# First cells of a fused mLSTM and gated MLP kernel: other PSUM banks for two products, another order on ScalarE, and cell 4's exponents between two weight joins

## The chip, the cores and the metric

The kernel runs on one core of one Trainium2 chip. The metric is the device time of one execution in microseconds. An execution is also recorded by the hardware profiler; the span of the recorded instructions is a little shorter than the time of that execution, and every position in the trace below is counted from the span's start. The five engines of a core have queues of their own and run side by side: PE (matrix products; its weight loads are a row of their own, PEld), DVE (VectorE), ACT (ScalarE), POOL (GpSimd) and SP (which here only issues DMAs). An engine works its instructions off in the order of its queue, and an instruction that waits for a semaphore holds up everything behind it on that engine.

## The reference

For batch 4, 8 heads, 768 steps and head size 40, an mLSTM cell is run step by step, and its output goes through an MLP whose gate is a cosine:

```python
m_new = np.maximum(f_gate[t] + m, i_gate[t])
f_stab, i_stab = np.exp(f_gate[t] + m - m_new), np.exp(i_gate[t] - m_new)
C = f_stab * C + i_stab * outer(v[t], k[t])
n = f_stab * n + i_stab * k[t]
y[t] = sigmoid(o_gate[t]) * (C @ q[t]) / np.maximum(np.abs(n @ q[t]), 1.0)
...
h = x @ w_in                  # x: y as (3072, 320); w_in (320, 2048)
out = (h * np.cos(h)) @ w_out # w_out (2048, 320)
```

## The kernel before

**Cells.** The recurrence is computed in chunks of 128 steps. A chunk of one batch entry is a cell: cell n is chunk n // 4 of batch entry n % 4, and there are 24. Inside a cell the decay between two steps is a 128x128 matrix per head, so that the cell becomes attention-like products. A cell's parts are functions that record instructions:

- `turn(n)` (L421) transposes q and k on PE into PSUM, and `turn_out(n)` (L432) copies both to SBUF, on ACT, or with k on DVE (L434, L436, L438).
- `decay_exponents(n)` (L370): DVE takes the exponents of all 8 heads from E, a 512 KB tile that SP loaded (`load_E`, L345), at L372; POOL puts the causal mask on it (L373). `decay(n)` (L380) takes the exponential on ACT (L381). Cells 0 and 1 get their exponents through PE instead: `wall_in` and `spread` write a mask and the maxima into PSUM banks (L352, L359).
- `scores(n)` (L440) multiplies k and q on PE, `weigh(n)` (L450) multiplies by the decay on DVE (L453, two instructions), `values(n)` (L466) multiplies by v on PE (L472), and `normalize(n)` (L525) makes z on DVE (L535 to L548).
- `weigh_k(n)` makes kw on POOL (L394). `seam(n)` (L569) transposes z into PSUM (px, L575) and forms the increment of the state (pu, L582); `seam_out(n)` (L590) copies px to xT, the MLP's input, and `state(n)` (L592) puts pu into the state (L596 copies it for cells 0 to 3). Both are ACT copies in the first four cells.

**The MLP.** Four cells make a chunk of 512 columns. `Up` (L603) multiplies it by two blocks of w_in: two products for each of two 128-row pieces (L617) and two for the last 64 rows (L620). `near` (ACT, L625), `rest` (DVE, L628), `sin` (ACT, L633) and `gate` (DVE, L637) make h cos h from it, and `down` multiplies by w_out (L750 in the first chunk, L693 later). The next `Up` reuses the two PSUM banks of the one before, so it waits for both gates.

**Weights.** They arrive as 64-bit numbers and are made into 32-bit ones: `parts` (ACT, L138 and L140) splits a piece and `join` puts it together (DVE, L144, L146, L148, then L149 on POOL or, with `nc.vector`, on DVE). The rounds of both_parts join the pieces as they need them. The first three pieces of w_in are joined in `first_cells`, the first piece of w_out in `cell_after_first` through `out_parts` and `out_join` (L890, L894).

**PSUM.** Eight banks: two of pool `ps_a` (tag "a", even cells), four of `ps_o` (tag "o", odd cells), two of `ps_u`. Tiles of one tag take its banks in turn, and a tile waits until the readers of the tile that had the bank are done. The two banks of `ps_u` are first `pw`, into which `warm(k)` (L759) writes k products of zeros that keep PE busy, and `pmu`, which holds the mask of cell 0; then they go to `Up`.

**Order.** Nothing reorders: under a manual schedule the order of the calls is the order on every engine. `first_cells` (L764) writes out cells 0 to 3 by hand. Then `both_parts(c, b)` (L899) does a round for each batch entry of a chunk: an `Up`, a cell's scores, `down` of the round before, the cell's values, another `Up`, and so on. In the first round `cell_after_first` (L874) is called inside the first `Up`, between its first and second pair of products: it turns cell 4 and takes its exponents, its decay and the first join of w_out. `gates_exp` (L259, two exponentials L261 on ACT and a DMA of the result to DRAM on POOL's queue, L262) and `gates_diagonal` (L264, one DVE product, L266) prepare what `gates_turn` (L269) gives to the later chunks.

Of the kernel before, what the change touches and what calls it, by code (L numbers as in the profile page):

```python
# [11 lines left out]
FP = mybir.dt.float32  # L12
# [17 lines left out]
def kernel(  # L30
# [22 lines left out]
    B, H, S, D = q.shape  # L53
    C = 128
    NC = S // C
    BH = B * H
    HP = H // 2
    D1 = D + 1
# [5 lines left out]
    NK = DM // 128  # L64
# [78 lines left out]
    def join(dst, hi, t, m, last=None):  # L143
        nc.vector.tensor_scalar(out=t.bitcast(FP), in0=t.bitcast(FP), scalar1=LEAST, scalar2=GREATEST,  # L144
                                op0=OP.max, op1=OP.min)
        nc.vector.tensor_scalar(out=t, in0=t, scalar1=5, scalar2=2, op0=OP.logical_shift_left,  # L146
                                op1=OP.logical_shift_right)
        nc.vector.scalar_tensor_tensor(out=t, in0=hi, scalar=TOP2, in1=t, op0=OP.bitwise_and, op1=OP.bitwise_or)  # L148
        (last or nc.gpsimd).tensor_tensor(out=dst.bitcast(I32), in0=t, in1=m, op=OP.add)  # L149
# [61 lines left out]
    def gates_in():  # L211
        nc.sync.dma_start(out=F0, in_=fg[:, 0:C])
        nc.scalar.dma_start(out=a0, in_=ig[:, 0:C])

    def later_gates_in():
        nc.sync.dma_start(out=F1.rearrange("r c s -> r (c s)"), in_=fg[:, C:])
        nc.sync.dma_start(out=a1.rearrange("r c s -> r (c s)"), in_=ig[:, C:])
# [41 lines left out]
    def gates_exp():  # L259
        for e in (eG, eW):  # L260
            nc.scalar.activation(out=e, in_=e, func=AF.Exp)  # L261
        nc.gpsimd.dma_start(out=G_d, in_=eG.rearrange("r c s -> r (c s)"))  # L262

    def gates_diagonal():  # L264

        nc.vector.tensor_tensor(out=dd, in0=ident[0:BH, 0:BH].unsqueeze(1).to_broadcast([BH, R - 1, BH]),  # L266
                                in1=eG[:, 0:R - 1, last].to_broadcast([BH, R - 1, BH]), op=OP.mult)
# [40 lines left out]
    def sigmoid(c, bs=slice(0, B)):  # L308
        o = sig[c][:, bs.start * DM:bs.stop * DM]
        nc.scalar.activation(out=o, in_=o, func=AF.Sigmoid)  # L310
# [51 lines left out]
    def psum_o():  # L362
        return ps_o.tile([128, HP, C], FP, name="pm", tag="o")

    def cols(n, j, width):
        c, b = divmod(n, B)
        return tab[:, c, j, ts(b, H)].unsqueeze(2).to_broadcast([128, H, width])


    def decay_exponents(n):  # L370
        E = Es[n]
        nc.vector.tensor_tensor(out=E, in0=E, in1=cols(n, 0, C), op=OP.subtract)  # L372
        nc.gpsimd.affine_select(out=E, in_=E, compare_op=OP.is_ge, fill=1.0e30, base=0,  # L373
                                pattern=[[0, H], [1, C]], channel_multiplier=-1)
# [16 lines left out]
    def weigh_k(n):  # L391
        if n < N - B:
            kw = p2.tile([128, H, D], FP, name="kw", tag="kw")
            nc.gpsimd.tensor_tensor(out=kw, in0=ks[n % NB][:, :, 0:D], in1=cols(n, 1, D), op=OP.mult)  # L394
            kws[n] = kw

    def psum(n):

        return (ps_o, "o") if n < B and n % 2 == 1 else (ps_a, "a")
# [32 lines left out]
    def turn_out(n, on_dve=True):  # L432
        qT, kT = qkT[n]
        nc.scalar.copy(out=qT, in_=pts[n][0])  # L434
        if on_dve:
            nc.vector.tensor_copy(out=kT, in_=pts[n][1])  # L436
        else:
            nc.scalar.copy(out=kT, in_=pts[n][1])  # L438
# [11 lines left out]
    def weigh(n):  # L450
        for j in range(2):
            w = Es[n].rearrange("p (a j) t -> p a j t", j=2)[:, :, j]
            nc.vector.tensor_tensor(out=w, in0=pss[n][j], in1=w, op=OP.mult)  # L453
# [12 lines left out]
    def values(n):  # L466
        pool, tag = psum(n)
        ph = pool.tile([128, H, D1], FP, name="ph", tag=tag)
        for j in range(2):
            for p in range(HP):  # L470
                h = 2 * p + j
                nc.tensor.matmul(ph[:, h], Es[n][:, h], vs[n % NB][:, h], start=True, stop=True)  # L472
        heads_of[n] = heads_of.get(n), ph
# [95 lines left out]
    def seam(n):  # L569

        pool, tag = psum(n)
        if n < TURNED:
            px = pool.tile([128, NK + 1, C], FP, name="px", tag=tag)
            for i in range(NK + 1):
                nc.tensor.transpose(px[:, i], ys[n][:, ts(i, 128)], ident)  # L575
            pxs[n] = px
        if n < N - B:

            pu = pool.tile([128, HP, D1], FP, name="pu", tag=tag)
            for p in range(HP):  # L580
                for j in range(2):
                    nc.tensor.matmul(pu[64 * j:64 * j + D, p], kws[n][:, 2 * p + j], vs[n % NB][:, 2 * p + j],  # L582
                                     start=True, stop=True)
            pus[n] = pu

    def seam_out(n):
        c, b = divmod(n, B)
        if b == 0:
            xT[c] = p2.tile([128, NK + 1, B, C], FP, name="xT", tag="xT")
        nc.scalar.copy(out=xT[c][:, :, b], in_=pxs[n])  # L590
# [166 lines left out]
    pw, pmu = (ps_u.tile([128, HP, C], FP, name=name, tag="up") for name in ("pw", "pmu"))  # L757
# [6 lines left out]
    def first_cells():  # L764
        nc.vector.memset(nil, 0.0)
        gates_in()
        nc.scalar.copy(out=ident_b, in_=ident)
        load(0, "qk")
        later_gates_in()
        load(1, "qk")  # L770
        load(0, "v")
        load_o(0, (0, 1))
        load(2, "qk")
        load_E(0)
        load_E(1)
        warm(9)
        gates_first()
        later_fills()
        gates_first_out()
        wall_in(0, 0, pmu)  # L780
        wall_in(0, 1, psum_o())
        spread(0, 0)
        decay_exponents_half(0, 0)
        turn(0)
        turn_out(0, False)
        gates_sums()
        spread(0, 1)
        decay_exponents_half(0, 1)
        decay(0)
        weigh_k(0)  # L790
        load_E(2)
        load(1, "v")
        load(3, "qk")
        load_o(0, (2, 3))
        load_E(3)
        load(2, "v")
        load(3, "v")
        pieces.extend(weights_in(0))
        wall_in(1, 0, psum_o())
        wall_in(1, 1, psum_o())  # L800
        gates_less_sums()
        spread(1, 0)
        decay_exponents_half(1, 0)
        scores(0)
        gates_maxima()
        turn(1)
        weigh(0)
        sigmoid(0, slice(0, 2))
        turn_out(1, False)
        spread(1, 1)  # L810
        decay_exponents_half(1, 1)
        gates_exponents()
        decay(1)
        weigh_k(1)
        values(0)
        normalize(0)
        scores(1)
        gates_exp()
        turn(2)
        turn_out(2, False)  # L820
        warm(2)
        seam(0)
        weigh(1)
        seam_out(0)
        state(0)
        load(B)
        decay_exponents(2)
        gates_diagonal()
        decay(2)
        weigh_k(2)  # L830
        values(1)
        load_E(B)
        outs.append((0, weights_out(0)))
        load_o(1, (0,))
        load_E(B + 1)
        normalize(1)
        scores(2)
        turn(3)
        sigmoid(0, slice(2, 4))
        seam(1)  # L840
        weigh(2)
        decay_exponents(3)
        turn_out(3)
        seam_out(1)
        values(2)
        decay(3)
        weigh_k(3)
        state(1)
        normalize(2)
        scores(3)  # L850
        pg = gates_turn()
        warm(1)
        seam(2)
        weigh(3)
        join(*parts(*pieces.pop(0)))
        pieces.extend(weights_in(1))
        load(B + 1)
        outs.extend((p, weights_out(p)) for p in range(1, 3))
        load_o(1, (1, 2, 3))
        seam_out(2)  # L860
        second = parts(*pieces.pop(0))
        state(2)
        gates_keep(*pg)
        values(3)
        normalize(3)
        warm(5)
        seam(3)
        join(*second, nc.vector)
        seam_out(3)
        join(*parts(*pieces.pop(0)), nc.vector)  # L870
        load_E(B + 2)
        state(3)

    def cell_after_first():  # L874

        turn(B)
        turn_out(B, False)
        decay_exponents(B)
        decay(B)
        weigh_k(B)  # L880
        out_join(*out_parts())

    spot = const.tile([1, 1], FP, name="spot")
    nc.gpsimd.memset(spot, 0.0)
# [5 lines left out]
    def out_parts():  # L890
        p, piece = outs.pop(0)
        return p, parts(*piece)

    def out_join(p, h, last=None):  # L894
        join(*h, last)
        if p + 3 < NF // 2:
            outs.append((p + 3, weights_out(p + 3)))
# [156 lines left out]
```

## Time and profile before

| What | Value |
|---|---|
| time, median of 5 runs (lowest, highest) | 538.93 us (538.17, 540.36) |
| time of the profiled execution | 538.37 us |
| its span | 536.4 us |
| mean granted clock of PE | 0.996 |
| PE busy over the span | 527.7 us |
| DVE, ACT, POOL busy | 363.6, 261.5, 167.6 us |
| first product of the first `Up` (L617) | 35.11 us |
| first product of the second `Up` | 48.05 us |
| SP's DMA issue of cell 4's E (L345) | 32.10 us |

A row of the timeline gives the start in us, the duration in us, the engine, the source line, the operation, output <- inputs with shapes, how many instructions are merged, and in brackets the idle time before the row with what ended it. Matmul ends are modelled, and a row can overlap the next by some tenths because the instructions are pipelined. "PEclk" in the table by stage is the granted clock of PE as a share of full speed.

### The profile page before, as it was taken

What the parts mean: (1) busy time and instruction counts of PE and PEld (TensorE: products, weight loads), DVE (VectorE), ACT (ScalarE), POOL (GpSimd) and SP (SyncE); (2) the same over time, 40 slices, a digit from 0 to 9 for tenths busy, and PEclk for the clock granted to TensorE, in tenths of its full rate; (3) what the DMA queues carried; (4) which work ended last, traced back from release to release, by engine and by line L of the source; (5) the groups of instructions that cost most, each with busy time, mean ns of one, the idle gap of its engine ahead of it and who ended that gap; (6) DMA issues with size and microseconds to landing.
All of it is one profiled execution on the core that took longest, in us unless ns stands there. A gap on an engine that the chain in (4) does not pass through costs nothing.

```text
span 536.4 us, 9941 instructions
## 1 busy us (share of the span) xinstructions
PE 527.7 (98%) x3634; PEld 333.5 (62%) x3634; DVE 363.6 (68%) x727; ACT 261.5 (49%) x416; POOL 167.6 (31%) x304
## 2 busy tenths in 40 slices
PE   9998999999999999999999999999999999999997
PEld 6864666665575666666666656656756756656555
DVE  5877678869687677777767777777876765422323
ACT  4869696765633445544436525427335332332312
POOL 5522433516353453223322422422222221212121
PEclk9998999999999999999999999999999999999999
DMA  9999986952266752166734076635074000010001
GB/s 138 211 221 234 241 214 175 194 113 48 71 132 137 163 113 57 51 138 144 157 94 90 12 177 133 139 86 123 6 179 112 7 15 11 6 50 0 2 0 49
DMA packets 134512, 56.86 MB, mean 106 GB/s; under 512 B 72080, under 2 KB 130528, under 8 KB 134464
## 3 DMA queue, kind: packets, MB, share of 16 engines
q1 hardware_dynamic: 134320, 56.04, 46.8%
q8 instruction: 28, 0.46, 0.4%
q0 software_dynamic: 96, 0.18, 0.2%
q14 instruction: 20, 0.16, 0.1%
q10 hardware_dynamic: 48, 0.02, 0.0%
HBM read 50.00 MB, written 6.21 MB: 105 GB/s over the span
## 4 chain that ended last, share of the span: by engine, by line
PE 82%; SPq 5%; DVE 4%; DMA 3%; ACT 2%; issue 2%; POOL 1%; DVEq 0%; POOLq 0%; ACTq 0%
PE po L693 32%; PE pup L617 28%; PE pup L620 9%; PE po L750 3%; PE hp L490 3%; PE ps L447 3%; SPq L329 2%; PE hp L484 2%; PE pu L582 1%; DMA E<-M_d 1%; SPq L300 1%; DMA qs<-in_q_dram 1%; SPq L129 1%; DVE n L628 1%; DVE E L453 1%
## 5 line engine op out<-in xcount | busy, mean ns | idle before, releaser
L617 PE MATMUL pup<-xT,w_in_sb 128*128 128x512 f32 x384 | 176.4, 602 | 1.8 <-DVE g L637 1.5
L625 ACT ACTIVATE n<-pup 128x512 int32<-128x512 f32 x96 | 52.0, 593 | 211.5 <-PE pup L620 211.5
L628 DVE SCALAR_TENSOR_TENSOR n<-pup,n 128x512 f32<-128x512 f32 x96 | 61.8, 686 | 122.8 <-ACT n L625 122.8
L693 PE MATMUL po<-w_out_sb,g 128*128 128x320 f32 (+1 forms) x480 | 118.6, 396 | 0.0
L617 PEld LDWEIGHTS pup<-xT,w_in_sb 128*128 128x128 f32 x384 | 70.3, 192 | 74.6 <-issue 63.7
L693 PEld LDWEIGHTS po<-w_out_sb,g 128*128 128x128 f32 x480 | 83.5, 190 | 36.7 <-issue 9.1
L676 POOL TENSOR_TENSOR sg<-g 128x128 f32<-128x128 f32 x80 | 36.7, 458 | 192.7 <-DVE g L637 191.3
L633 ACT ACTIVATE n<-n 128x512 f32<-128x512 f32 x96 | 58.9, 630 | 12.4 <-DVE n L628 12.4
L637 DVE SCALAR_TENSOR_TENSOR g<-pup,n 128x512 f32<-128x512 f32 x96 | 61.6, 683 | 2.5 <-ACT n L633 1.2
L620 PE MATMUL pup<-xT,w_in_l 64*128 64x512 f32 x192 | 54.2, 641 | 0.0
L373 POOL TENSOR_SCALAR_AFFINE_SELECT E<-E 128x1024 f32<-128x1024 f32 x19 | 20.8, 1093 | 101.3 <-DVE E L372 80.3
L693 PE MATMUL po<-T,sg 128*128 128x160 f32 x240 | 39.4, 300 | 0.0
L620 PEld LDWEIGHTS pup<-xT,w_in_l 64*128 64x128 f32 x192 | 14.4, 184 | 36.4 <-issue 35.6
L750 PE MATMUL po<-w_out_sb,g 128*128 128x320 f32 x128 | 36.6, 439 | 0.1
L693 PEld LDWEIGHTS po<-T,sg 128*128 128x128 f32 x240 | 34.8, 190 | 0.2
L412 DVE STREAM_TRANSPOSE t<-qs 128x512 f32<-128x512 f32 x32 | 32.7, 1103 | 0.0
L381 ACT ACTIVATE E<-E 128x1024 f32<-128x1024 f32 x21 | 22.2, 1057 | 18.7 <-POOL E L373 17.1
L447 PEld LDWEIGHTS ps<-t,t 40*128 40x128 f32 (+1 forms) x384 | 25.1, 188 | 9.7 <-issue 9.4
L453 DVE TENSOR_TENSOR E<-ps,E 128x512 f32<-128x512 f32 x48 | 30.6, 679 | 0.0
L750 PEld LDWEIGHTS po<-w_out_sb,g 128*128 128x128 f32 x128 | 23.7, 190 | 9.7 <-POOL w_out_sb L149 0.3
L447 PE MATMUL ps<-t,t 40*128 40x128 f32 (+1 forms) x384 | 25.8, 274 | 0.0
L888 ACT ACT_TABLE_LOAD x19 | 24.4, 1283 | 0.3
(146 smaller groups left out, 639.2 us busy)
## 6 DMA issues: line engine op xcount, KB each, us to landing
E<-M_d SPq DMA_DIRECT2D x22, 512.0 KB
bits<-in_moe_w_in_dram SPq DMA_DIRECT2D x40, 128.0 KB
bits<-in_moe_w_out_dram SPq DMA_DIRECT2D x8, 640.0 KB
room<-G_d SPq DMA_DIRECT2D x32, 128.0 KB
ks<-in_k_dram SPq DMA_DIRECT2D x24, 160.0 KB
vs<-in_v_dram SPq DMA_DIRECT2D x24, 160.0 KB
qs<-in_q_dram SPq DMA_DIRECT2D x32, 80.0 KB
qs<-in_k_dram SPq DMA_DIRECT2D x32, 80.0 KB
```

The costliest lines, as they stand in the source:

```text
L412: nc.vector.transpose(out=dst.rearrange("r p (t x) -> r p x t", x=T4), in_=src.rearrange("r p (x d) -> r p x d", x=T4)[:, :, :, 0:32])
L447: nc.tensor.matmul(ps[j][:, p], kT[r, p], qT[r, p], start=True, stop=True)
L453: nc.vector.tensor_tensor(out=w, in0=pss[n][j], in1=w, op=OP.mult)
L617: nc.tensor.matmul(pu, w_in_sb[:, i, ts(block(f2, e), 128)], x(i), start=(i == 0), stop=False)
L620: nc.tensor.matmul(pu, w_in_l[r, f2], x(NK, r), start=False, stop=True)
L625: nc.scalar.activation(out=self.n[e], in_=self.pu[e], func=AF.Copy, bias=0.25)
L628: nc.vector.scalar_tensor_tensor(out=self.n[e].bitcast(FP), in0=self.pu[e], scalar=0.25, in1=self.n[e], op0=OP.add, op1=OP.subtract)
L633: nc.scalar.activation(out=r, in_=r, func=AF.Sin, scale=TWO_PI_DOWN)
L637: nc.vector.scalar_tensor_tensor(out=g, in0=self.pu[e], scalar=TWO_PI, in1=self.n[e].bitcast(FP), op0=OP.mult, op1=OP.mult)
L676: nc.gpsimd.tensor_tensor(out=S[:, i], in0=x, in1=y, op=op)
L693: nc.tensor.matmul(out, g, w, start=(f2 == 0 and first), stop=end, skip_group_check=True)
L750: nc.tensor.matmul(po[c][b], gs[c, f][:, ts(b, C)], w_out_sb[:, f], start=(f == 0), stop=(f == NF - 1))
```

## The change

It edits two functions and the order of calls in two others.

- `seam`: for cells 0 to 2, px goes to the bank `pmu` and pu to the start of the bank `pw`, instead of to tiles of the cell's pool. Cell 3 keeps its tiles, which stand before the first `Up`.
- `first_cells`: the sigmoid of batch entries 0 and 1 comes behind the two copies of `turn_out(1)` instead of in front of them. `gates_exp` comes behind cell 2's decay and `weigh_k(2)` instead of in front of `turn(2)`, and `gates_diagonal` behind `turn_out(3)` instead of behind `decay_exponents(2)`.
- `decay_exponents(B)`, cell 4's exponents, comes between the second and the third join of w_in in `first_cells` instead of behind `turn_out(B)` in `cell_after_first`; there `out_parts` comes in front of cell 4's decay, instead of behind `weigh_k(B)`.

No computation is added or taken away. On SP's queue nothing changes place; on POOL's, the DMA of L262 comes behind cell 2's mask and kw.

```diff
         if n < TURNED:
-            px = pool.tile([128, NK + 1, C], FP, name="px", tag=tag)
+            px = pmu[:, 0:NK + 1] if n < B - 1 else pool.tile([128, NK + 1, C], FP, name="px", tag=tag)
...
-            pu = pool.tile([128, HP, D1], FP, name="pu", tag=tag)
+            if n < B - 1:
+                pu = pw.rearrange("r p t -> r (p t)")[:, 0:HP * D1].rearrange("r (p d) -> r p d", p=HP)
+            else:
+                pu = pool.tile([128, HP, D1], FP, name="pu", tag=tag)
...
         weigh(0)
+        turn_out(1, False)
         sigmoid(0, slice(0, 2))
-        turn_out(1, False)
...
         scores(1)
-        gates_exp()
         turn(2)
...
         decay_exponents(2)
-        gates_diagonal()
         decay(2)
         weigh_k(2)
+        gates_exp()
         values(1)
...
         turn_out(3)
+        gates_diagonal()
         seam_out(1)
...
         join(*second, nc.vector)
+        decay_exponents(B)
         seam_out(3)
         join(*parts(*pieces.pop(0)), nc.vector)
...
         turn_out(B, False)
-        decay_exponents(B)
+        first_out = out_parts()
         decay(B)
         weigh_k(B)
-        out_join(*out_parts())
+        out_join(*first_out)
```

## The prediction

> **What bounds the kernel now.** The share of busy time comes first, then the table by stage, then who PE waited for:
>
> ```profile
> PE 527.7 (98%) x3634; PEld 333.5 (62%) x3634; DVE 363.6 (68%) x727; ACT 261.5 (49%) x416; POOL 167.6 (31%) x304
> ...
> 45.00:50.00 5.00, 3.47 (x17) 2.32 (x17) 4.83 (x10) 4.26 (x7) 1.65 (x2) 0.77 1.11 161
> 50.00:55.00 5.00, 5.00 (x28) 2.05 (x28) 2.66 (x8) 4.97 (x7) 1.98 (x3) 0.89 1.03 313
> 55.00:60.00 5.00, 5.00 (x33) 3.63 (x28) 4.55 (x10) 3.32 (x8) 1.88 (x3) 1.00 1.03 253
> ...
> PE pup L617 <- DVE g L637: 1.5, 1, 1.5
> ```
>
> The columns behind the stretch are busy us of PE, PEld, DVE, ACT, POOL, then the granted clock, DMA share and GB/s. From 50 us on PE is full, so what the change can win or lose is the time at which that full stretch stands. PE's last real wait is 1.5 us before the second `Up` at 48.05, and behind it the clock is halved for a while: the eight L617 there take 5.21 us, those at 60.61 take 3.44, so 1.77 us. The timeline of cells 1 to 4 shows the chains in front (ACT, DVE, then PE):
>
> ```profile
> 16.16 1.06 ACT L381 ACTIVATE E<-E 128x1024 f32<-128x1024 f32 x1
> 17.18 1.36 ACT L261 ACTIVATE room<-room 32x640 f32<-32x640 f32 x2
> ...
> 21.85 1.06 ACT L381 ACTIVATE E<-E 128x1024 f32<-128x1024 f32 x1 [1.07 <-POOL E L373]
> ...
> 22.92 1.28 ACT L310 ACT_TABLE_LOAD   x1
> ...
> 27.26 1.06 ACT L381 ACTIVATE E<-E 128x1024 f32<-128x1024 f32 x1
> ...
> 28.43 1.28 DVE L453 TENSOR_TENSOR E<-ps,E 128x512 f32<-128x512 f32 x2
> ...
> 37.81 1.22 DVE L372 TENSOR_TENSOR E<-E,tab 128x1024 f32<-128x1024 f32 x1
> ...
> 41.99 0.49 DVE L144 TENSOR_SCALAR wt<-wt 128x640 f32<-128x640 f32 x1 [2.96 <-ACT wt L138]
> ...
> 43.79 1.28 DVE L453 TENSOR_TENSOR E<-ps,E 128x512 f32<-128x512 f32 x2
> ...
> 44.57 1.95 PE L472 MATMUL ph<-vs,E 128*128 128x41 f32 x16 [0.62 <-issue]
> ```
>
> ACT works without a gap from 21.85 to 30, and cell 3's decay (27.26) is what cell 3's weighing (28.43) waits for. In cell 4, DVE idles 2.96 us for the parts of w_out, which ACT takes only after cell 4's decay; the join then pushes the weighing to 43.79, though the scores ended at 41.61. That is the hole worth filling.
>
> **Banks.** px(0) waited 0.39 us for ACT's copy (ends 19.01) and pu(0) for the next (19.50). In the banks of zeros they follow the warm products: px at 18.6, pu at 19.1, values(1) at 19.5 instead of 20.07, where the second half of weigh(1) ends (19.51) anyway: 0.57 earlier. normalize(1) starts at 21.5, weigh(2) at 23.05 (decay(2) ends 22.91), values(2) end at 26.27 instead of 26.84. New waits: warm(1) for the copies of state(1), warm(5) for those of state(2), because both write `pw`. Behind the first stand px(2), pu(2) and values(3).
>
> **Sigmoid.** Cell 1's copies move from 13.79 to 12.4, but PE reads them at 16.05, after values(0): no gain. ACT now idles for the transposes (to 12.35), so decay(1) starts at 16.8, not 16.16, and ends at 17.85. DVE hides that, busy with z(0) until weigh(1) starts at 18.24; without that cover it costs 0.6.
>
> **Gates.** The 1.36 us of L261 leave a place where they delayed px(0), and enter one where ACT is full: decay(2) cannot start before 21.85 (its mask), so all behind it is 1.26 us later: copy of q(3) ends 26.8, decay(3) 29.6, state(1) 30.06. scores(3) move by 0.1. L266 (0.27) leaves an idle place of DVE and meets POOL's mask of cell 3 (about 25.5 to 26.6), which blocks it (next part): normalize(2) starts at 26.9 as before, and the 0.57 is gone. weigh(3) is at 29.6 instead of 28.43, warm(1) at 30.1 instead of 29.27, px and pu follow, values(3) at 31.18 instead of 30.35: **0.83 late**, and so are normalize(3) and the first `Up`, at 35.95. L262's issue (0.55) waits on POOL behind kw(2), at 23.6; POOL is idle until 25.5, and G is read at 100 us.
>
> **Cell 4.** The second join ends at 37.17 (36.34 + 0.83). L372 then waits for its E: the trace's landing events have the last of it at 37.3 (bounds: no wait, or 37.81, when L372 ran before); I take 37.4, so it ends at 38.6. POOL's mask starts at 38.7. The third join, which stood in front of L372, now stands beside that mask and kw(4) (0.72). No row shows this pair of join and L373; the nearest are these:
>
> ```profile
> 61.34 0.84 POOL L149 TENSOR_TENSOR w_in_l<-wt,wm 128x256 int32<-128x256 int32 x1 [1.08 <-DVE wt L148]
> 61.63 0.90 DVE L146 TENSOR_SCALAR wt<-wt 128x640 int32<-128x640 int32 x1
> ...
> 97.43 1.09 POOL L388 TENSOR_SCALAR_AFFINE_SELECT E<-E 128x1024 f32<-128x1024 f32 x1 [1.15 <-ACT E L387]
> 97.56 1.31 DVE L540 TENSOR_TENSOR y<-o,hs 128x320 f32<-128x320 f32 x1
> ```
>
> L146 takes 0.49 alone and L540 0.44: each stood until POOL's instruction had ended. Bounds: nothing, or the whole mask and kw, 1.8 us. I take 1.55, L144, mask, L146, kw, L148, L149 in turn: the join, 1.64 us alone, ends at 41.75 instead of 40.2. PE needs it for L620 (39.58 before; 40.42 by the 0.83): **L620 at 41.8**, scores end 2.03 later, at 43.83.
>
> ACT: copies to 39.45, parts of w_out to 40.9 (their bits landed at 39.1), decay(4) to 41.9, `near` behind L620. The join of w_out ends on DVE at 43.6, under the scores. So weigh(4) starts at 43.9, 0.09 late. Then rest, L372 of cell 5 and the gates follow as now, and the second `Up` starts at 48.14. But PE's own work has moved right up to it: scores end, pq and six warm products (2.34), values (1.95), at 48.1. No idle 1.5 us, and, I take it, no half clock: this `Up` ends at 52.7 instead of 54.32.
>
> PE would then be 1.6 early, but ACT and DVE are not: from the first sin (45.70) ACT runs back to back to `near` at 54.71, DVE from there to the gates at 58.75 and 60.04. All of that is 0.09 late. The third `Up` needs both gates; its second product stood at 60.88 and now can stand at 60.04 + 0.09 + 0.04 = 60.17: **0.71 early**. From there ACT waits for PE (3.06 us at 65.14), w_out's next join ends at 65.16 for a product at 65.22, and the DMA waits at 88 to 95 hang on DVE's joins, which move along. So 0.71 reaches the end: 538.37 - 0.71 = 537.66 in the profiled execution, which lies 0.56 under the median; **538.2** on the median.
>
> **A rule against the row.** The half clock begins at 47.7, after no gap of PE longer than 1.53 us. The Trainium skill, TensorE: Matmul & The Clock Gate, "What's actually happening", lets the clock fall after an idle window of about 3.4 us. By it the changed kernel has no half clock anywhere; by the row it may, since sparse work with gaps was enough.
>
> **Rivals.**
> 1. *The join is not blocked.* For: L144 at 102.90 kept its 0.42 beside L567. Against: the rows above. The join ends at 40.2, L620 at 40.42, weigh(4) at 42.5, 1.29 early; the third `Up`'s second product stands at 58.79: 2.09 early, 536.8.
> 2. *The half clock stays* behind 48.14: PE arrives at 60.55, 0.1 late: 539.0. For: it came after sparse products there. Against: six warm products now lie in that window.
> 3. *Slower: a half clock in the first cells.* warm(1) waits from 29.2 to 30.1 and warm(5) from 33.16 to 33.6, among small products. If that halves the clock for one stretch, the work from 30.1 to 34.9 takes up to 1.77 more. The first `Up` is then at 37.7, the second join at 38.94, the blocked third at 43.3, weigh(4) 1.66 late and the third `Up`'s second product at 61.75: 0.87 late, 539.8. It decides from about 0.8 us of such loss on, which uses up the 0.71. With the wait of two banks for copies delayed by 1.26, this is the change's own price.
>
> **Numbers.** Forecast 0.36, rival 1 0.32, rival 2 0.10, rival 3 0.18, else 0.04. Low end: rival 1 with PE alone as the limit (second `Up` at 46.8, done at 51.3, 3.0 early), 536.0. High end: rivals 2 and 3 together (second `Up` at 49.7, half clock to 56.0, 1.7 late), 540.6. A measurement can tell 0.3%, 1.6 us. Faster takes most of rival 1 and a little else, 0.30; slower half of rival 3 and a little, 0.12; same 0.58.
>
> **What would show it.** px(0) right behind the warm products; L261 in front of the sigmoid's table load and decay(3) near 28.5; warm(1) waiting for L600; the first `Up` at 36; L372 waiting for DMA until 37.4; L146 over 1 us; L620 near 41.8; no bracket before the second `Up` and a clock of 1.00 there. If E lands early, or L146 takes 0.29, rival 1 holds; if the first `Up` is past 37, rival 3.

## The result, and the profile after

The changed kernel takes 538.25 us (median of 54 executions, 536.28 to 542.03), the kernel before 539.81 us beside it (94 executions, 537.04 to 542.55): a ratio of 0.9978, 95% interval 0.9969 to 0.9987, or 1.2 us. The ratio is that of the means, 538.68 and 539.86; the medians lie 1.6 us apart. I had forecast 0.7 us of gain. That 538.2 and 538.25 nearly meet is partly luck: I had put my 0.7 on a median of five, 538.93, and over 94 executions this median is 0.9 higher. The profiled execution took 536.53 us (span 534.8) against 538.37 (536.4).

The table by stage of the changed kernel, over the same stretches as in the prediction (behind the stretch: its length, busy us of PE, PEld, DVE, ACT and POOL, the granted clock, DMA share, GB/s), and who PE waited for:

```profile
45.00:50.00 5.00, 4.68 (x25) 3.19 (x23) 4.79 (x11) 4.83 (x7) 1.09 (x1) 1.00 1.13 177
50.00:55.00 5.00, 5.00 (x33) 2.63 (x32) 2.33 (x7) 4.97 (x8) 2.16 (x3) 1.00 1.13 303
55.00:60.00 5.00, 4.67 (x21) 2.95 (x20) 4.83 (x11) 3.33 (x8) 1.96 (x2) 1.00 1.01 270
```

```profile
PE ph L472 <- DVE E L453: 0.9, 1, 0.9
PE pup L624 <- DVE w_in_l L149: 0.6, 1, 0.6
PE pw L766 <- ACT st L600: 0.5, 2, 0.4
PE pup L621 <- DVE g L641: 0.3, 1, 0.3
```

The wait of 1.5 us before the second `Up` and the half clock behind it are gone (PE 4.68 instead of 3.47 busy between 45 and 50, clock 1.00 instead of 0.77). Two new waits are there, for the third join (0.6) and for the copies of the state (0.5). The 0.9 us ahead of cell 0's values were 0.5 in the profile of before; that wait differs from profile to profile, whatever the edit (see rival 3 below). The timeline of cells 2 to 4:

```profile
22.81 1.35 ACT L261 ACTIVATE room<-room 32x640 f32<-32x640 f32 x2
...
28.50 1.06 ACT L381 ACTIVATE E<-E 128x1024 f32<-128x1024 f32 x1
...
29.69 1.28 DVE L453 TENSOR_TENSOR E<-ps,E 128x512 f32<-128x512 f32 x2
...
30.10 0.38 PE L766 MATMUL pw<-nil 128*128 128x512 bf16 x1 [0.16 <-ACT st L600]
...
35.92 1.96 PE L621 MATMUL pup<-xT,w_in_sb 128*128 128x512 f32 x4 [0.22 <-ACT xT L594]
...
37.08 1.22 DVE L372 TENSOR_TENSOR E<-E,tab 128x1024 f32<-128x1024 f32 x1
...
38.53 1.07 DVE L146 TENSOR_SCALAR wt<-wt 128x256 int32<-128x256 int32 x1
...
41.08 1.13 PE L624 MATMUL pup<-xT,w_in_l 64*128 64x512 f32 x4 [0.61 <-DVE w_in_l L149]
...
43.20 1.29 DVE L453 TENSOR_TENSOR E<-ps,E 128x512 f32<-128x512 f32 x2 [0.38 <-PE ps L447]
...
47.48 3.70 PE L621 MATMUL pup<-xT,w_in_sb 128*128 128x512 f32 x8 [0.32 <-DVE g L641]
```

Cell 4's weighing starts at 43.20 instead of 43.79, the second `Up` at 47.48 instead of 48.05, and its eight products take 3.70 us instead of 5.21. The gates end at 59.50, and the third `Up`, whose second product waits for them, starts in the changed kernel (L621) and before (L617) at:

```profile
58.21 1.29 DVE L641 SCALAR_TENSOR_TENSOR g<-pup,n 128x512 f32<-128x512 f32 x2
...
59.04 3.24 PE L621 MATMUL pup<-xT,w_in_sb 128*128 128x512 f32 x7
```

```profile
60.45 1.88 PE L617 MATMUL pup<-xT,w_in_sb 128*128 128x512 f32 x4
```

Its second product stands at 59.55 instead of 60.88. At 118 us the products are 1.34 us ahead, at 134 us 1.55, as the end is (1.6); nothing here explains the 0.2 us in between.

Not all of this is as I saw it. In this execution a half clock stands in the first cells, where the profile of before had none:

```profile
12.76:16.17 3.41, 2.51 (x23) 2.28 (x23) 2.53 (x5) 3.36 (x4) 2.33 (x5) 1.00 1.18 249
16.17:19.58 3.41, 3.41 (x24) 3.19 (x25) 3.31 (x9) 1.66 (x3) 1.66 (x2) 0.50 1.12 158
```

So values(1) ran at 20.96, not at 19.5. It can't be laid to the change: e6 and e7 below, whose first cells are those of before, have a half clock at the same place in their profiles (16.72 and 16.36). This half clock, and how many of its kind an execution has, turned out to be the other half of the story.

### The profile page after: what moved, and what is told of

Same layout as the page of the kernel before. It is cut to its first block, busy times and chain, and to the rows that moved or that the text cites. A ratio compares the mean times of both kernels' runs of the same rounds, so it can differ in the third digit from the quotient of the medians.

```text
span 534.8 us, 9942 instructions
## 1 busy us (share of the span) xinstructions
PE 527.2 (99%) x3634; PEld 334.3 (63%) x3634; DVE 365.6 (68%) x727; ACT 261.8 (49%) x416; POOL 167.7 (31%) x304
## 4 chain that ended last, share of the span: by engine, by line
PE 92%; ACT 3%; DMA 2%; DVE 1%; issue 0%; POOL 0%; SPq 0%; ACTq 0%; POOLq 0%
PE po L697 32%; PE pup L621 30%; PE pup L624 9%; PE po L754 6%; PE ps L447 4%; PE hp L490 3%; DMA bits<-in_moe_w_in_dram 2%; PE hp L484 2%; PE ph L472 2%; PE pu L586 1%; PE pt L428 1%; PE pw L766 1%; PE pq L462 0%; ACT L381 0%; ACT E L381 0%
## 5 line engine op out<-in xcount | busy, mean ns | idle before, releaser
L621 PE MATMUL pup<-xT,w_in_sb 128*128 128x512 f32 x384 | 175.0, 598 | 0.7 <-DVE g L641 0.3
L621 PEld LDWEIGHTS pup<-xT,w_in_sb 128*128 128x128 f32 x384 | 69.7, 190 | 72.8 <-issue 63.4
L624 PE MATMUL pup<-xT,w_in_l 64*128 64x512 f32 x192 | 54.2, 641 | 0.6 <-DVE w_in_l L149 0.6
L624 PEld LDWEIGHTS pup<-xT,w_in_l 64*128 64x128 f32 x192 | 14.4, 184 | 37.1 <-issue 35.6
```

Source lines behind the costliest of these rows:

```text
L621: nc.tensor.matmul(pu, w_in_sb[:, i, ts(block(f2, e), 128)], x(i), start=(i == 0), stop=False)
L624: nc.tensor.matmul(pu, w_in_l[r, f2], x(NK, r), start=False, stop=True)
```

## A second view: how many half-clock stretches an execution has

Every execution is listed with its mean granted clock. A stretch of 3.41 us at half clock lowers it by 0.0032, so the number of stretches is (1 - clock) x 536 / 1.7, rounded. In the kernel before, the time rises by 1.07 us with each (a line fitted through 105 executions: medians of 538.8, 539.6, 541.1 and 541.8 us with one to four). A comparison of two medians therefore mixes two things: work that moved, and stretches that came or went. The table has both; n is 12 except for the changed kernel (54) and before (105, all of them beside the experiments). The ratios are not quotients of these medians.

| Kernel | median us | ratio to before, 95% interval | mean stretches | with 4 or more |
|---|---|---|---|---|
| before | 539.8 to 540.0 | | 2.25 | 9 of 105 |
| changed | 538.25 | 0.9978, 0.9969 to 0.9987 | 2.26 | 17 of 54 |
| e1, cell 4 alone | 538.16 | 0.9972, 0.9959 to 0.9984 | 1.33 | 1 |
| e2, banks alone | 540.77 | 1.0012, 0.9991 to 1.0034 | 3.42 | 7 |
| e8, gates alone | 540.87 | 1.0015, 0.9996 to 1.0035 | 3.08 | 6 |
| e3, gates undone | 538.81 | 0.9987, 0.9965 to 1.0009 | 2.58 | 4 |
| e4, exponents undone | 537.94 | 0.9974, 0.9948 to 1.0000 | 2.67 | 4 |
| e7, parts first alone | 539.39 | 0.9989, 0.9971 to 1.0006 | 2.25 | 3 |
| e6, hole filled | 538.73 | 0.9985, 0.9967 to 1.0003 | 1.33 | 0 |
| e10, zeros to the other bank | 539.62 | 0.9981, 0.9957 to 1.0005 | 2.67 | 5 |
| e11, three undone | 538.49 | 0.9978, 0.9956 to 0.9999 | 2.33 | 3 |
| e12, first hole filled | 539.54 | 0.9990, 0.9972 to 1.0009 | 2.08 | 2 |
| e13, v first | 539.57 | 0.9992, 0.9971 to 1.0012 | 2.92 | 6 |
| e14, cell 4 and first hole | 538.50 | 0.9974, 0.9957 to 0.9990 | 0.75 | 0 |

## The experiments

My theory after the result: the cell-4 edit wins all of the gain, since it closes PE's hole of 1.53 us and with it a half clock; the edits of the first cells win nothing. The rival: the banks' 0.57 us counts too, and the gates or the exponents cost something that could be taken back.

**e1, cell 4 alone.** The kernel before, with the cell-4 edit only:

```diff
         join(*second, nc.vector)
+        decay_exponents(B)
...
         turn_out(B, False)
-        decay_exponents(B)
+        first_out = out_parts()
         decay(B)
         weigh_k(B)
-        out_join(*out_parts())
+        out_join(*first_out)
```

> The kernel before with the last edit alone: cell 4's exponents between the two joins, and the parts of w_out in front of cell 4's decay. Banks, sigmoid and gates stay. The first Up then stays at 35.1 us and the second join ends at 36.3. Theory A (the third join stands still beside POOL's mask and kw, and behind the second Up the gates on DVE and ACT set the time): the third join ends near 40.4, weighing of cell 4 near 42.5 instead of 43.79, the third Up 2.0 us earlier than before, so 1.5 to 2.0 us faster than the kernel before and 0.5 us or more faster than the changed kernel. Theory B (cell 4's E is what counts, and it lands at 37.3 as in the profile of before): L372 waits a microsecond, the third join ends at 41.4 and the kernel is 1.1 us faster than before. Theory C (a join that is not blocked): 2.9 us faster.

Measured: 0.9972 (0.9959 to 0.9984), 1.5 us. The low end of theory A; B's 1.1 us lies inside the interval too, C's 2.9 us does not. The mean number of stretches falls by 0.92, from 2.25 to 1.33; among executions with one stretch each, e1 is at 537.97 (6) and before at 538.77 (19). As far as the intervals tell, this edit alone gives what the whole change gives. Its profile has two windows of half clock in the first cells (21.61 to 28.43), though banks and gates are as before.

**e2, banks alone.** The kernel before, with px and pu of cells 0 to 2 in the banks of masks and zeros:

```diff
-            px = pool.tile([128, NK + 1, C], FP, name="px", tag=tag)
+            px = pmu[:, 0:NK + 1] if n < B - 1 else pool.tile([128, NK + 1, C], FP, name="px", tag=tag)
...
-            pu = pool.tile([128, HP, D1], FP, name="pu", tag=tag)
+            if n < B - 1:
+                pu = pw.rearrange("r p t -> r (p t)")[:, 0:HP * D1].rearrange("r (p d) -> r p d", p=HP)
+            else:
+                pu = pool.tile([128, HP, D1], FP, name="pu", tag=tag)
```

> The kernel before with the first edit alone: px and pu of cells 0 to 2 in the banks of the mask and of the zero products. Theory A: values(1) starts at 19.5 instead of 20.07, but the five warm products now wait for the copies of state(2) (end 32.9), so px(3) stands where it stood and the first Up starts at 35.1 as before: 0.0 us, within 0.3. Rival: the warm products' waits cost nothing, and the 0.45 us that px(2) wins reach the end.

Measured: 1.0012 (0.9991 to 1.0034), not to be told from no change, with 3.42 stretches. In its trace the hole of cell 4 is as before (1.53 us), and the half clock behind it lasts two windows (47.53 to 54.36) instead of one:

```profile
48.66 6.52 PE L620 MATMUL pup<-xT,w_in_sb 128*128 128x512 f32 x8 [1.53 <-DVE g L640]
```

**e3, gates undone.** The changed kernel, with `gates_exp` and `gates_diagonal` at their old places.

```diff
+        gates_exp()
         turn(2)
...
+        gates_diagonal()
         decay(2)
         weigh_k(2)
-        gates_exp()
...
         turn_out(3)
-        gates_diagonal()
```

> The changed kernel with gates_exp and gates_diagonal back at their old places; banks, sigmoid and cell 4 stay as changed. Theory A: decay(3) is at 27.3 again and the first Up at 35.1 to 35.3 instead of 35.9; everything to the third Up follows, so 0.5 to 0.8 us faster than the changed kernel and 1.8 to 2.2 faster than before. Rival (E of cell 4 is the limit, the 0.83 us of delay were hidden by its landing): the same time as the changed kernel, L372 waiting for DMA.

Measured: 0.9987 (0.9965 to 1.0009), inconclusive beside the changed kernel's 0.9978. In its profile cell 3's decay waits for POOL's mask and not for ACT's queue. But two stretches (15.57 to 22.40) fell into the first cells, so the decay stands at 29.67 and the first `Up` at 37.25, and the expected places can't be read from it.

**e4, exponents undone.** The changed kernel, with cell 4's exponents back behind the third join:

```diff
         join(*second, nc.vector)
-        decay_exponents(B)
         seam_out(3)
...
         turn_out(B, False)
+        decay_exponents(B)
         first_out = out_parts()
```

> The changed kernel with cell 4's exponents behind the third join again (their old place on DVE); the parts of w_out stay in front of cell 4's decay. Theory A: the third join is no longer blocked (L146 0.29 us) and L620 starts at 40.4 instead of 41.1, but now POOL's mask and kw block the join of w_out, so cell 4's weighing starts within 0.3 us of where it does in the changed kernel (43.2) and the time is the same. Rival (only the third join matters): weighing at 42.5, 0.7 us faster than the changed kernel.

Measured: 0.9974 (0.9948 to 1.0000). Its timeline shows what rival 1 of the prediction (a join that isn't blocked) is worth:

```profile
37.45 0.29 DVE L146 TENSOR_SCALAR wt<-wt 128x256 int32<-128x256 int32 x1
...
40.46 1.13 PE L624 MATMUL pup<-xT,w_in_l 64*128 64x512 f32 x4
40.61 0.81 DVE L144 TENSOR_SCALAR wt<-wt 128x640 f32<-128x640 f32 x1 [0.70 <-ACT wt L138]
...
43.12 1.28 DVE L453 TENSOR_TENSOR E<-ps,E 128x512 f32<-128x512 f32 x2
...
47.39 3.70 PE L621 MATMUL pup<-xT,w_in_sb 128*128 128x512 f32 x8 [0.85 <-DVE g L641]
```

The third join is free (L146 takes 0.29) and L624 waits for nothing. But POOL's mask and kw now block the next join, that of w_out (L144 takes 0.81 where it took 0.49), which ends on DVE at 43.2, and weigh(4) stands behind it on DVE: 43.12 here, 43.20 in the changed kernel. In these two profiles, each with one early stretch (16.59 here), the two orders are worth the same; only who is late differs. The executions, 0.9974 and 0.9978, can't tell them apart.

**e7, parts first alone.** The kernel before, with `first_out` taken ahead of cell 4's decay and nothing else.

```diff
         decay_exponents(B)
+        first_out = out_parts()
         decay(B)
         weigh_k(B)
-        out_join(*out_parts())
+        out_join(*first_out)
```

> The kernel before, with only one line of the change: the parts of the first piece of w_out are taken ahead of cell 4's decay; cell 4's exponents stay behind the third join of w_in. Theory A (the parts' place is what wins, the exponents' place wins nothing because it only moves POOL's block from one join to another): the third join keeps 0.29 us at L146, the product of L620 stays near 39.6, weigh(4) starts near 42.4 instead of 43.79, the second Up near 46.8 without a half clock; ratio 0.9965 to 0.9972, at least as good as the whole cell-4 edit (0.9972). Theory B (both moves are needed): weigh(4) stays at 43.5 or later and the ratio is 0.999.

Measured: 0.9989 (0.9971 to 1.0006), the number of theory B. The profile speaks for A: from the first to the second `Up` it is 11.40 us (36.05 to 47.45), against 12.94 before and 11.56 in the changed kernel and in e1, and the third `Up` starts at 59.01 (59.04 in the changed kernel). But this execution is the slowest of the twelve (541.61): PE sits idle for 1.73 us up to 83.89, a half clock follows at 84.62, and the `Up` at 98.89 is 2.6 us behind that of before. Whether this comes with the edit, one profile can't say. So neither what the parts' place wins alone nor what the exponents' place adds is shown over many executions.

**e6, hole filled.** The kernel before, with six products of zeros behind cell 4's values in the first round.

```diff
+                if begin:
+                    warm(6, psum_o())
```

> The kernel before, with six products of zeros added behind the values of cell 4, where PE stood idle for 1.53 us ahead of the second Up. No product of the reference is left out. Theory A (the one behind the prediction): the half clock of 47.72 to 51.13 goes, the second Up still starts near 48.1 and ends near 52.6 instead of 54.32, but the third Up then waits for the gates, which ACT and DVE deliver no earlier, so its second product stands at about 60.1 instead of 60.88: 0.7 to 0.8 us of gain, ratio 0.9986. Theory B (the half clock alone is what the cell-4 edit won): the gain is that of the cell-4 edit alone, ratio 0.997. Theory C (added products only add): ratio 1.002 or more.

Measured: 0.9985 (0.9967 to 1.0003); A had 0.9986. The second `Up` stands 12.95 us behind the first, as before, but at full clock (3.70 us for its eight products). It has 1.33 stretches, as e1 has. By the two ratios the half clock alone is worth about half of what the cell-4 edit wins, and the other half is that ACT and DVE reach the gates earlier; this is an estimate, since the interval of e6 holds 1.

**e10, zeros to the other bank.** The changed kernel, with the zeros of cells 2 and 3 in `pmu`, so that they don't wait for the copies of the state:

```diff
-        warm(1)
+        warm(1, pmu)
...
-        warm(5)
+        warm(5, pmu)
```

> The changed kernel, with the one product of zeros ahead of cell 2's seam and the five ahead of cell 3's seam written to the bank pmu instead of pw, so that they no longer wait for the copies of the state (0.16 and 0.38 us of PE's idle time in the changed kernel). Theory A (rival 3 of the prediction: these waits make the clock fall in the first cells, and that is what takes back part of the gain): the executions with four or more stretches of half clock, 17 of 54 in the changed kernel, become as rare as in the kernel before (3 of 35), and the ratio falls to 0.9965. Theory B (the weak window is the one ahead of 16 us, where nothing waits for a bank; which window counts is set by when the grid of 3.41 us falls): the share stays near 1 in 3 and the ratio near 0.9978; the first Up stays at 35.9, since cell 3's copy to xT is still last there.

Measured: 0.9981 (0.9957 to 1.0005), and 5 of 12 executions with four or more stretches. Theory A, my rival 3 in its literal form, falls: without these waits the stretches are no rarer. Its profile is one without a half clock before 41 us, and shows three other waits:

```profile
24.83 1.95 PE L472 MATMUL ph<-vs,E 128*128 128x41 f32 x16 [2.30 <-DMA vs<-in_v_dram]
...
37.60 1.23 DVE L372 TENSOR_TENSOR E<-E,tab 128x1024 f32<-128x1024 f32 x1 [1.63 <-DMA E<-M_d]
...
41.62 2.08 PE L624 MATMUL pup<-xT,w_in_l 64*128 64x512 f32 x4 [2.33 <-DVE w_in_l L149]
```

PE reached the values of cell 2 at 22.5 and waited 2.30 us for v of cell 2. But in this execution, as in those of e13 and e1, the cells began early: cell 0's weighing stands at 11.75 (11.93 and 12.12 there) instead of 13.4 to 13.6 in all others, while the loads came when they always come. So some 1.7 us of the 2.30 are this execution's own; e12, with the usual start, waits 0.82. The window with this wait (20.85 to 24.26, PE 1.69 us busy) had a full clock behind it. L372 does wait for its E, as the prediction had it, at 37.6, and PE then waits 2.33 us for the third join; behind that window (1.37 us busy) the clock is halved at 41.33.

**e11, three undone.** e10 with the gates back as in e3 and the exponents back as in e4.

> The changed kernel with the gates' exponentials and diagonal back at their old places, cell 4's exponents back behind the third join, and the products of zeros of cells 2 and 3 in the bank pmu. Theory A (the gates' and the exponents' moves lose, the banks' and the parts' moves win): where no half clock falls into the first cells, the first Up starts at 34.6 to 35.1, L620 near 39.2, the second Up near 46.6; the ratio is 0.996 or less, under that of every kernel so far. Theory B (the second Up is bound by the landing of w_out's bits near 39.1 and by ACT's chain from there): the second Up stays at 47.2 or later, and the ratio is 0.9972 to 0.998, as in the changed kernel.

Measured: 0.9978 (0.9956 to 0.9999). B's ratio, though the interval also holds A's 0.996. The profile can't tell what holds the second `Up`, because two stretches of half clock (15.78 to 22.61) put the first one at 37.33.

**e8, gates alone.** The kernel before, with `gates_exp` behind `weigh_k(2)` and `gates_diagonal` behind `turn_out(3)`, as in the change.

> The kernel before, with only the gates' exponentials behind cell 2's decay and weigh_k, and the gates' diagonal behind turn_out(3). Theory A (the prediction's step on the gates: decay(3) near 28.5, weigh(3) near 29.6, everything behind it 0.83 us late): where no half clock falls into the first cells, L261 ends near 24.2, decay(3) stands at 28.5 instead of 27.26, values(3) near 31.2 instead of 30.35, the first Up near 35.95 instead of 35.11; over the executions 0.8 us more, ratio 1.0015. Theory B (ACT has room for it, since cell 3's mask on POOL waits for its E in any case): decay(3) near 27.3, no change, ratio 1.000.

Measured: 1.0015 (0.9996 to 1.0035), the number of theory A, though its interval holds 1. Six of twelve executions have four stretches, and the profile caught one of them. First the rows, then PE's windows of 3.41 us (columns as in the table by stage):

```profile
22.82 1.35 ACT L261 ACTIVATE room<-room 32x640 f32<-32x640 f32 x2
...
26.88 1.52 PE L447 MATMUL ps<-t,t 64*128 64x128 f32 x16 [0.55 <-DVE F L266]
...
28.52 1.06 ACT L381 ACTIVATE E<-E 128x1024 f32<-128x1024 f32 x1
...
32.72 3.64 PE L472 MATMUL ph<-vs,E 128*128 128x41 f32 x16
```

```profile
24.12:27.53 3.41, 2.86 (x42) 2.69 (x38) 3.34 (x8) 3.34 (x6) 2.07 (x3) 1.00 0.91 255
27.53:30.94 3.41, 3.00 (x24) 2.41 (x21) 2.13 (x6) 3.36 (x6) 0.00 (x0) 0.50 0.74 186
30.94:34.36 3.42, 3.42 (x28) 2.81 (x27) 1.41 (x3) 2.60 (x7) 1.27 (x1) 0.50 1.06 180
34.36:37.77 3.41, 3.41 (x14) 2.38 (x14) 1.27 (x6) 0.53 (x3) 0.00 (x0) 0.50 0.93 263
37.77:41.18 3.41, 3.41 (x23) 2.09 (x22) 3.13 (x9) 1.61 (x5) 0.00 (x0) 0.50 1.16 274
41.18:44.60 3.42, 3.42 (x15) 1.78 (x13) 1.75 (x3) 1.41 (x3) 1.46 (x2) 1.00 0.93 213
```

L261 puts ACT's copy of q(3) at 26.24 (24.98 before), and PE, which had cell 2's values done early here, waits 0.55 us for it ahead of scores(3). (The bracket names L266; the copy ended at 26.82, 0.06 ahead of the product.) The window in front has a single gap of 0.55 us. Behind it the clock is halved for four windows, though PE has no idle time at all in three of them. The first `Up` is at 39.79 instead of 35.11.

**e12, first hole filled.** The changed kernel, with three products of zeros ahead of cell 0's values:

```diff
         weigh_k(1)
+        warm(3)
         values(0)
```

> The changed kernel, with three products of zeros (0.66 us) added in front of cell 0's values, where PE stood idle for 0.90 us waiting for weigh(0). Theory A (the clock falls after a stretch of 3.41 us in which PE did too little, and the first such stretch, 12.76 to 16.17 in the changed kernel, is this hole): a half clock near 16 us becomes rare, executions without any stretch of half clock become common, the share with four or more falls below 1 in 6, and the ratio falls to 0.997 or less. Theory B (products of zeros in this hole don't help, or the counted stretches lie elsewhere): the counts stay as they are, with 17 of 54 at four or more, and the ratio is 0.9978 or higher by the 0.3 us that the added products cost where there is no hole.

Measured: 0.9990 (0.9972 to 1.0009). Half of A holds: 3 of 12 executions have no stretch (1 of 54 without the zeros), and 2 of 12 have four or more. But the time doesn't fall. The profile, with a full clock up to 29.64, is the cleanest view of the change's first cells:

```profile
18.52 0.49 PE L576 MATMUL pmu<-ident,z 128*128 128x128 f32 x3
...
19.37 1.98 PE L472 MATMUL ph<-vs,E 128*128 128x41 f32 x16
...
25.05 1.95 PE L472 MATMUL ph<-vs,E 128*128 128x41 f32 x16 [0.82 <-DMA vs<-in_v_dram]
...
28.51 1.06 ACT L381 ACTIVATE E<-E 128x1024 f32<-128x1024 f32 x1
...
30.10 0.58 PE L766 MATMUL pw<-nil 128*128 128x512 bf16 x1 [0.91 <-ACT st L600]
...
31.96 3.64 PE L472 MATMUL ph<-vs,E 128*128 128x41 f32 x16
```

px(0) and values(1) are where the banks were to bring them. Then PE waits 0.82 us for v of cell 2, in a window with a full clock behind it, and 0.91 us for the state's copy behind the gates; the half clock, three windows long, begins inside this second wait, at 29.64.

**e13, v first.** The changed kernel, with cell 2's v ahead of cell 3's E on SP's queue.

```diff
         load_o(0, (2, 3))
+        load(2, "v")
         load_E(3)
-        load(2, "v")
```

> The changed kernel, with cell 2's load of v put ahead of cell 3's E on SP's queue. In the kernel before, this v lands at 24.64 and the values of cell 2 start at 24.86; over the ten traces so far it lands at 23.8 to 24.9. Theory A (the banks' 0.57 us were never to be had, because this v would have been late next): v lands 0.8 to 2 us earlier, the values of cell 2 don't wait for it in any execution, and the ratio falls to 0.997. Theory B (cell 3's E takes its place as the late one, near 24.6 to 25): the wait moves to DVE's L372 of cell 3, and the ratio stays at 0.9975 to 0.9985.

Measured: 0.9992 (0.9971 to 1.0012), 6 of 12 executions with four stretches. What B describes, with a ratio above B's range, which the interval holds: v lands at 21.62, E of cell 3 at 25.84, and PE's wait moves from the values of cell 2 to the scores of cell 3. The cells began 1.5 us early here (see e10), which lengthens both waits:

```profile
25.86 1.23 DVE L372 TENSOR_TENSOR E<-E,tab 128x1024 f32<-128x1024 f32 x1 [3.15 <-DMA E<-M_d]
...
27.84 1.94 PE L447 MATMUL ps<-t,t 64*128 64x128 f32 x16 [3.22 <-DVE t L436]
```

In these profiles (e10, e12, e13) the first cells meet the loads near 24 to 26 us, whichever of the two comes last.

**e14, cell 4 and first hole.** e1 with the three products of zeros of e12.

> The kernel before with the change's cell-4 edit alone and the three products of zeros in front of cell 0's values. Theory A (as for the fill in the changed kernel): fewer stretches of half clock than with the cell-4 edit alone (2, 6, 3, 0, 1 executions with 0, 1, 2, 3, 4 of them), most at none; ratio 0.9965 or less, the best so far. Theory B: the counts and the ratio stay at those of the cell-4 edit alone, 0.9972.

Measured: 0.9974 (0.9957 to 0.9990), with 0.75 stretches, the fewest of all, and none in 5 of 12 executions. A is right that the stretches become fewer and wrong on the time, which is that of e1. The profile, at full clock throughout, shows a reason:

```profile
38.23 1.22 DVE L372 TENSOR_TENSOR E<-E,tab 128x1024 f32<-128x1024 f32 x1 [1.86 <-ACT t L434]
...
42.25 1.13 PE L620 MATMUL pup<-xT,w_in_l 64*128 64x512 f32 x4 [2.56 <-DVE w_in_l L149]
```

The first `Up` starts at 35.13, but E of cell 4 lands only at 38.14 (by the landing events; the copy that the bracket names ends at the same time and is no input of L372). L372 waits for it, the third join stands behind L372 and POOL's mask, and PE waits 2.56 us. In this execution, what a full clock saves in the first cells is given back at this load.

No version beats the changed kernel by more than the intervals allow: e1, e4 and e14 lie at 0.9972 to 0.9974, the change at 0.9978.

## Why the prediction was right, and where it was not

**Cell 4: mechanism right, one term mis-sized.** The third join is blocked by POOL, L624 waits for it, the second `Up` follows at full clock and the gates set the third `Up`. The failed term is the time of the third join, "ends at 41.75": it ended at 41.03. Of the 0.72, 0.30 is L372, which I put at 37.4 behind the landing of its E and which ran at 37.08 without a wait, since in this execution E landed at 36.38; SP had issued it at 31.26, not at 32.10. Nearly all of the other 0.42 is the block: from L144 to L149 the join took 2.82 us, 1.18 over its 1.64 alone, not 1.55. The mask lengthened L146 by 0.78, but kw(4) (39.43 to 40.19) only lengthened L148 by 0.40, where I had counted all of its 0.72. The prediction's own rows said as much: L146 and L540 ended 0.35 us behind POOL's instruction, less than their 0.49 and 0.44 alone, so they hadn't stood to its very end. What follows is early by the same amount: L624 0.72, weigh(4) 0.70, the second `Up` 0.66, and the second product of the third `Up` 0.62 (59.55, not 60.17). So this execution gained 1.3 us there instead of 0.71. The landing was no constant to be read from one trace: over all 14 it is 36.4 to 38.7, with issues between 31.04 and 33.55 and 5.0 to 6.4 us from issue to landing. In e10 and e14 the wait that I had forecast is there, at 37.60 and 38.23.

**Rival 1 (join not blocked) did not occur:** L146 took 1.07 us. Its price, weigh(4) 1.29 us ahead of before, isn't tested. e4 comes nearest: there the third join isn't blocked, because L372 and the mask come behind it, and weigh(4) is at 43.12, 0.67 ahead of before and 0.08 ahead of the changed kernel, since the block passes on to w_out's join.

**Banks: places right, gain not there.** At full clock px(0) is at 18.52 and values(1) at 19.37 (e12; predicted 18.6 and 19.5). The step failed behind that, at "values(2) end at 26.27": v of cell 2 lands at 24.64 in the trace of before, and its values start at 24.86. Two tenths of the 0.57 were there at most, and I hadn't looked at this landing. I wrote the 0.57 off anyway, but for the gates.

**Gates: right up to warm(1).** e8 and e12 have cell 3's decay at 28.52 and 28.51 (28.5 predicted) and the weighing at 29.61 and 29.60 (29.6); in e12 warm(1) is at 30.10 (30.1). The first `Up` at 35.95 is not shown: both have a half clock from 27.5 or 29.6 on. In the changed kernel's own profile the same places (28.50, 29.69, 30.10, 35.92 for 35.95) are no proof: there the early half clock delays as much, as in e6 and e7, where the gates are not moved and the first `Up` is at 35.99 and 36.05.

**Sigmoid: no gain, as said,** though not measured by itself: weigh(1) starts at 18.24 before and after.

**Rival 3 (half clock in the first cells): real, its cause open.** Over the kernels that have the banks' or the gates' edit, 54 of 150 executions have four stretches or more; over those with neither, 13 of 153. I had blamed the waits of the zeros for the state's copies. e10 takes those away, and the share does not fall. The profiles show stretches of two kinds in the first cells. One stands near 16 us and is not the change's: in the fourteen profiles PE waits 0 to 1.21 us ahead of cell 0's values; in the seven with 0.57 us or more, e6 and e7 among them, a half clock begins at 15.6 to 16.8, and in the other seven none does. The other kind is three or four windows long and begins at 27.5 to 29.6, in e8, e12 and e13, which all have the gates' edit. There PE waits for what isn't earlier: the copy of q(3) (e8), the state's copy behind the gates (e12), E of cell 3 (e13). (e1's, two windows from 21.61 on, is of neither kind.) That such a wait makes the long stretch is argued, not shown: in e10 a wait of 2.30 us had a full clock behind it.

The cell-4 edit alone takes away some 0.92 stretches per execution, and in the whole change as many others come: 2.25 before, 2.26 after. The rule that the prediction set against the row, a clock that falls only after an idle window, would, read strictly, have allowed none of those in the profiles, the end of the span aside, where PE has finished: the window in front of a half clock has 0.20 us busy in e13 and 1.37 to 2.96 in all others. With as many stretches after as before, the 1.2 us that are left come, by this count, from the work that moved; the executions with one stretch each agree: 538.77 before (19), 537.41 after (26).

What stays open: what makes the long stretches; how the banks' and the gates' edits share them (twelve executions each are too few to tell 7, 6 and 4 apart); and whether the parts' place alone (e7) would do without the exponents' move.

## What to carry to other kernels

Before an edit that starts work earlier is credited, look up when each input of that work lands, and look in more than one trace: here v of cell 2 and E of cell 4 had a margin of 0.2 and 0.5 us, and over the traces the landings vary by 1.2 and 2.3 us, the issues included. An early engine in front of a late load only waits. On PE a half clock may follow, but need not: behind the wait of 3.22 us in e13 the clock was halved for four windows, behind that of 2.30 us in e10 for none. Look also at when an execution begins its work: three of fourteen began the cells 1.3 to 1.7 us early, and their waits for loads are longer by that. Where single executions differ by about 1 us, sort them by the mean granted clock first, and compare those with the same number of half-clock stretches.

## What the runs showed of the hardware

- The half clock comes in whole windows of 3.41 us (lengths of 3.41, 6.83, 10.24 and 13.65 us), on a grid that is fixed within an execution and differs between executions: in e2 at 16.81 and 47.53, nine windows apart; in e7 at 16.36 and 84.62, twenty. The Trainium skill, TensorE: Matmul & The Clock Gate, "What's actually happening", says that the window runs freely, which agrees. It lets the clock fall after an idle window; in e8 it fell after a window with 2.86 us of 3.41 busy and no gap over 0.55 us, and the measurement decides.
- PE's busy share alone doesn't decide: in e10 a window with 1.69 us busy (20.85 to 24.26) and in e12 one with 2.58 (22.82 to 26.23) had a full clock behind them, in e12 one with 2.96 (26.23 to 29.64) a half one. In e8 two windows without idle time (30.94 to 37.77), filled by small products and products of zeros, did not bring the clock back; it came back behind the window in which the first `Up` began (39.79), and so it did in e12 and e13 (39.03, 40.56). This is no rule: in the changed kernel's own profile one window of small products (16.17 to 19.58) was enough.
- DVE's L146 takes 0.29 us alone and 1.07 beside POOL's mask, ending 0.14 us behind it. This agrees with the Trainium skill, SBUF — State Buffer, "Who interferes with whom", by which GpSimd and a DVE instruction in a two-port mode block each other for a whole instruction, whichever issues first. No run here shows which mode L146 was in.
